# A Fourier mixing and SwiGLU kernel: rising rows turned by copies inside DRAM, the long set in blocks of four rows, and a new table of units

## The chip, the core and the metric

The kernel runs on one core of a Trainium2 chip. Its engines each take their instructions in order: TensorE (PE, matmuls, with its weight loads shown as PEld), VectorE (DVE), ScalarE (ACT), GpSimd (POOL), and SyncE (SP), which here only issues DMAs. ACT and POOL issue a few DMAs too. Matmul results land in PSUM, everything else lies in SBUF (128 partitions) or in DRAM. The metric is the device time of one execution in microseconds (us); less is better.

## What is computed

```python
def _attn_ref(x):                       # x: 8 x 3008 x 256, float32
    X = np.fft.fft(x, axis=1)
    X = np.fft.fft(X, axis=2)
    return X.real.astype(np.float32)

def _moe_ref(x, w_gate, w_val, w_out):  # x: 24064 x 256; w_gate, w_val: 256 x 1536; w_out: 1536 x 256
    g = x @ w_gate
    silu = g * (1.0 / (1.0 + np.exp(-g)))
    val = x @ w_val
    return (silu * val @ w_out).astype(np.float32)
```

The second function gets the 8 x 3008 rows of the first.

## The kernel before

**The mathematics.** The input is real, so output row k and its mirror 3008 - k come from the same two numbers: an even part P and an odd part Q, as P + Q and P - Q. The transform along the 256 columns is folded into the weights (tables `CD` and `SDt`, which give `Wp` and `Wq` from the gate and value weights; `Wm` holds the multiple of `Wq` that turns a plus sum in PSUM into the mirror's sum). The transform along the 3008 rows is halved several times: rows that rise from a quarter's start are added to rows that fall from its end. POOL does these additions (`fold_steps`, L171 to L205), and what is left is a product with the tables `Tab` (`transform_parts`, L1394).

**Sets of rows.** Of every quarter of a batch (752 rows) 188 pairs rise and 188 fall. 128 pairs make the long set A (buffer `XA`, 128 partitions x 8 x 2 x 256 float32; slots 0 to 3 for the four rising quarters, 4 to 7 for the falling ones) and 60 pairs the short set C (buffer `XC`, two batches in its two halves). There is one buffer of each, so a set of a later batch is loaded when the one before it is folded. A falling row's address runs against its partner's. The partitions are therefore filled in blocks: within a block of `LA` (or `LC`) rows the rising pairs go up, and the blocks themselves go down. A falling quarter is one DMA (`down_set`, L142), and a rising set takes one DMA for each block (`up_block`, L140 and L155), to 8 partitions at a time for A (16 DMAs) and 4 for C (15). The tables follow the order of rows (`m_cols`, `putA`), which is why `LA` appears there too. Batch 1 is special: its short set is spread over both halves of `XC` (L164; L169 is a copy from `XC` to `XC`), one parity of the pairs in each, so that six folding steps do for it where a full buffer takes twelve. Its long set's buffer first holds raw weights and the odd tables (`Wraw`, `rrO`), so the loads wait for the readers of these.

**Tiles and units.** 12032 columns of P and Q make 24 tiles, of 480, 512, 512, 480, 512, 512, then seventeen of 512, and one of 320. Each tile has 12 units, one for each 128 columns of the 1536. A unit makes a plus gate and a plus value and, by a further matmul into the same PSUM banks, the mirror's gate and value (L972). ACT takes the Silu (L1084, L1156, L1159), and DVE or POOL the products (`hp` at L1186 and L1192, `hm` for the mirror at L1183, two units at a time on POOL). `hp` and `hm` go to the output product (L1236), whose result ACT evicts (L1243) and SP stores (L1249).

**Kinds of units.** `KINDS` has a row for each tile and a digit for each unit (`w`: both signs' products whole, on DVE, in the first tile and the start of the second). Bit 1 (seeded): ACT writes the row term into PSUM before the value matmul (`v`, L1045) and copies the even value out (`es`, L1107); without it DVE does both in one instruction (`es`, L1109). Bit 2 (split gate): DVE makes the even gate (L1088) and the mirror gate (L1152), and the gate takes two matmuls; without it three. Digit 4 and up: ACT copies the value (`pp`, L1189) and POOL makes the plus product (L1192) instead of DVE (L1186); from 8 up POOL makes the mirror value too (L1195).

**The order of the work.** A planner inside the kernel (`Sched`) lists every operation behind the setup with an engine, a cost and a due time, plays it through and emits each engine's instructions in the order that it finds. Due times are TensorE's running sum plus a shift for each kind of operation (`SHIFT`) and a correction for each tile and kind (`BIAS_ROWS`, 24 rows of 17 numbers). So a change of costs, loads or corrections changes the order on all engines. Loads go to SP in small lots, a few at every unit, mixed with the stores and with the two DMAs that spread a tile's row term over the partitions (`br`, `bc`).

Of the kernel before, what the change touches and what calls it, by code (L numbers as in the profile page):

```python
# [12 lines left out]
F32 = mybir.dt.float32  # L13
# [6 lines left out]
def kernel(  # L20
# [8 lines left out]
    nc = tc.nc  # L29
    B, M, D = x.shape  # L30
    Dff = moe_w_gate.shape[1]
    P = 128
# [3 lines left out]
    R = M // 4  # L36
# [16 lines left out]
    NCR = GH - P  # L53
# [52 lines left out]
    XC = const.tile([P, 8, 2, D], F32, name="XC")  # L106
# [24 lines left out]

    JA, JC = P - LA + 1, GH - LC + 1

    C1_EARLY = 6
    C1_ORDER = "uuduuduuduuduumuueuueuece"
    A1_ORDER = "uuuuduuuuduuuuduuuud"

    def load_a(b, q):
        X3 = XA.rearrange("p a q d -> p a (q d)")
        res = ([lambda h=h: q.dma_start(out=X3[LA * h:LA * (h + 1), 0:4, :],  # L140
                                         in_=up_block(b, JA - LA * h, LA)) for h in range(NA)] +
                [lambda a=a: q.dma_start(out=X3[:, 4 + a, :], in_=down_set(b, a, JA, LA, NA)) for a in range(4)])  # L142
        return in_order(A1_ORDER, u=res[:NA], d=res[NA:]) if b == 1 else res

    def in_order(order, **todo):
        todo = {k: list(v) for k, v in todo.items()}
        return [todo[k].pop(0) for k in order]

    def load_c(b, q):

        X3 = XC.rearrange("p a q d -> p a (q d)")
        p0 = 64 * (b % 2)
        pm = p0 + NCR
        r = slice(p0, p0 + NCR)
        ups = [lambda h=h: q.dma_start(out=X3[p0 + LC * h:p0 + LC * (h + 1), 0:4, :],  # L155
                                       in_=up_block(b, JC - LC * h, LC)) for h in range(NC_)]
        mid = [lambda: q.dma_start(out=XC[pm:pm + 1, 0:4, 1],
                                   in_=rows_at(b, 0, [[R * D, 1], [R * D, 4], [1, D]]))]
        if b != 1:
            return ups + [lambda a=a: q.dma_start(out=X3[r, 4 + a, :], in_=down_set(b, a, JC, LC, NC_))  # L160
                          for a in range(4)] + mid

        def down(a, k):
            q.dma_start(out=XC[0:NCR, 4 + a, 0] if k else XC[r, 4 + a, 0],  # L164
                        in_=rows_at(b, R * (a + 1) - 2 * JC + k, [[2 * LC * D, NC_], [-2 * D, LC], [1, D]]))

        downs = [[lambda a=a, k=k: down(a, k) for a in range(4)] for k in range(2)]
        return in_order(C1_ORDER, u=ups, d=downs[0], e=downs[1], m=mid,
                        c=[lambda: q.dma_start(out=XC[0:NCR, 0:4, 1], in_=XC[r, 0:4, 0])])  # L169
# [82 lines left out]
    q = nc.sync  # L252
# [104 lines left out]
    sc = 2.0 * math.pi * (1.0 - 2e-7)  # L357
# [28 lines left out]
    def load_w(c, only):  # L386
        for i, src in ((0, moe_w_gate), (1, moe_w_val)):
            if i not in only:
# [13 lines left out]
                        in_=rows_at(0, 0, [[2 * R * D, 2], [R * D, 2], [1, D]]))  # L402
# [141 lines left out]
    for hi in range(2):  # L544
        q.dma_start(out=X3c[64 * hi + NCR:64 * hi + 64, :].rearrange("p (c d) -> p c d", d=D),
                    in_=zeros[64 * hi + NCR:64 * hi + 64].unsqueeze(1).to_broadcast([64 - NCR, 16, D]))
    loads_c1 = load_c(1, q)
    for load in loads_c1[:C1_EARLY]:
        load()
# [142 lines left out]
    A1_LOAD = 8  # L692
    ROW_1 = 12
    ROW_2 = 24
    ROW_3 = 35
    LOAD_AT = 2
# [45 lines left out]
    )  # L742
    BIAS = {(t, k): v for t, row in enumerate(BIAS_ROWS) for k, v in zip(SHIFT, row)}
# [11 lines left out]
    W_AT = (0.0, 2.0, 3.2, 4.6)  # L755
# [164 lines left out]
    def pool_us(n):  # L920
# [9 lines left out]
        "06ww20001013",  # L930
        "031303160011",
        "000010312133",
        "010210112012",
        "10110b103133",
        "001601031052",
        "300171700001",
        "331213005030",
        "010271031001",
        "34130b310300",
        "01b300700101",  # L940
        "21312101b300",
        "001371310011",
        "32120011b212",
        "10130b135030",
        "000135003170",
        "033170001011",
        "213b21011200",
        "103b10319610",
        "4030b13300b0",
        "616404563200",  # L950
        "143034169230",
        "706150233313",
# [21 lines left out]
    S = Sched()  # L974
# [310 lines left out]
    for b in range(2, B, 2):  # L1285
        u = slot[(b, 0)] - 1
# [6 lines left out]
    act_at = {}  # L1293
    spread_at = {}
    loads = []

    def run_loads(n):
        for what, k, fn in loads[:n]:
            up = k < (NA if what[0] == "A" else NC_)
            r, w, us, ring = [], [((what[0],), k)], 0.4 if up else 0.62, 0.57 if up or what[0] == "C" else 1.14  # L1300
            if what == ("A", 1):
                r = [(("C",), C1_ORDER.rindex("u"))]
                us, ring = (0.42, 0.75) if A1_ORDER[k] == "u" else (0.75, 1.1)
            if what == ("C", 1):
                us, ring = (0.48, 0.75) if C1_ORDER[k] == "u" else (0.95, 1.0)
                if C1_ORDER[k] == "c":
                    r = [(("C",), j) for j, o in enumerate(C1_ORDER) if o == "u"]
            S.add("SP", us, fn, r=r, w=w, after=[(("A",), "pre" if A1_ORDER[k] == "d" else "preW")] if what == ("A", 1) else [],
                  lat=2.5, ring=ring)
        del loads[:n]  # L1310
# [4 lines left out]
    def fold_step(what, i, unit):  # L1315
        kind, b = what
        q, j = (1, i) if what == ("C", 1) else divmod(i, 6)
        if i == 0:
            run_loads(max((k + 1 for k, (w_, _, _) in enumerate(loads) if w_ == what), default=0))
# [14 lines left out]
        r = {0: [((kind,), k) for k in range(40)], 1: [(tmp, "F")], 2: [(tmp, "F")], 3: [(tmp, "E"), (tmp, "O")],  # L1334
# [4 lines left out]
        if q == 1 and j == 0:  # L1339
            act_at.setdefault(max(unit + LOAD_AT, 15), []).append(what)  # L1340
# [6 lines left out]
    def load_next(what):  # L1347
        kind, b = what
        if kind == "A":
            if b + 1 < B:  # L1350
                loads.extend((("A", b + 1), k, fn) for k, fn in enumerate(load_a(b + 1, nc.sync)))
        else:
            b = b // 2 * 2 + 2
            if b < B:
                loads.extend((("C", b), k, fn) for k, fn in enumerate(load_c(b, nc.sync) + load_c(b + 1, nc.sync)))
# [248 lines left out]
    for k in range(C1_EARLY):  # L1604
        S.add("DMA", 0.01, lambda: None, w=[(("C",), k)], lat=2.0)
# [3 lines left out]
    S.add("DMA", 0.01, lambda: None, w=[(("pq", 0), "Q")], lat=0.1)  # L1609
# [7 lines left out]
    for i, u in enumerate(units):  # L1617
        t, f = u
# [3 lines left out]
        if i == 1:  # L1622
            loads.extend((("C", 1), k, fn) for k, fn in enumerate(loads_c1) if k >= C1_EARLY)
        if i == A1_LOAD:
            loads[0:0] = ((("A", 1), k, fn) for k, fn in enumerate(load_a(1, nc.sync)))
# [41 lines left out]
    S.run({'DVE': 1.6, 'ACT': 1.0, 'POOL': 1.4, 'PE': 0.0, 'SP': 2.0})  # L1667
# [30 lines left out]
```

## Time and profile before

| | us |
|---|---|
| median of three runs | 599.71 |
| lowest and highest | 597.59, 600.29 |
| the profiled execution | 600.4 |
| its span, first to last instruction | 598.6 |

| engine | busy in the span | instructions |
|---|---|---|
| PE | 587.0 (98%) | 3953 |
| DVE | 570.3 (95%) | 1064 |
| ACT | 557.4 (93%) | 1080 |
| POOL | 527.8 (88%) | 486 |

The hardware profiler recorded one execution. A row of a group names the line, the engine, the operation, what is written and read, how often, the busy time, the mean of one in ns, and the idle time just before such instructions with what ended it. A row of the waits names the engine and line that waited, what released it, the total in us, the number of times and the longest. A row of the timeline has the start, the duration, engine, line, operation and operands. In the table by stretches each engine's busy time is followed by its number of instructions, and at the end stand TensorE's granted clock, the mean busy share of 16 DMA engines and GB/s. Some matmul records are missing, and the end of a matmul is modelled.

### The profile page before, as it was taken

How to read it: one execution, taken by the hardware profiler on the slowest of the kernel's cores; microseconds unless marked ns; L12 is line 12 of the kernel's file. 1: busy time of each engine (PE TensorE's matmuls, PEld its weight loads, DVE VectorE, ACT ScalarE, POOL GpSimd, SP SyncE). 2: the span in 40 equal slices, each digit the busy share in tenths (PEclk: the TensorE clock that was granted, in tenths of full speed). 3: DMA queues.
4: the chain of work that ended last, by engine and by line, in shares of the span. 5: the costliest groups of instructions: out<-in, count | busy, mean ns of one | idle time of the engine just before them, and what ended most of it. 6: DMA issues, size and time to landing. Idle time of an engine off the chain costs nothing.

```text
span 598.6 us, 12468 instructions
## 1 busy us (share of the span) xinstructions
PE 587.0 (98%) x3953; PEld 389.2 (65%) x4012; DVE 570.3 (95%) x1064; ACT 557.4 (93%) x1080; POOL 527.8 (88%) x486
## 2 busy tenths in 40 slices
PE   7999999999999999999999999999999999999997
PEld 5456666666666666666666666666666666666686
DVE  8989999999999999999999999999999999999993
ACT  8778989989998999999999999999999999999995
POOL 8977999999899999998999998897986868687772
PEclk9999999999999999999999999999999999999999
DMA  9956347454715523454127122046221202111212
GB/s 247 150 110 115 109 121 141 132 140 117 178 46 107 136 70 113 123 129 138 57 55 166 46 62 82 19 115 161 63 64 37 65 19 80 48 46 53 60 54 81
DMA packets 51082, 57.65 MB, mean 96 GB/s; under 512 B 7283, under 2 KB 38439, under 8 KB 51017
## 3 DMA queue, kind: packets, MB, share of 16 engines
q1 hardware_dynamic: 47433, 53.91, 35.2%
q0 software_dynamic: 3216, 2.36, 2.8%
q8 instruction: 31, 0.51, 0.4%
q10 hardware_dynamic: 368, 0.59, 0.3%
q14 instruction: 34, 0.28, 0.2%
HBM read 29.43 MB, written 24.65 MB: 90 GB/s over the span
## 4 chain that ended last, share of the span: by engine, by line
PE 71%; ACT 8%; DMA 6%; DVE 4%; POOL 3%; issue 3%; SPq 1%; ACTq 0%; POOLq 0%; DVEq 0%
PE o L1236 30%; PE g L972 19%; PE v L972 16%; DMA XA<-in_x_dram 5%; ACT sv L1159 2%; PE o L1394 2%; PE g L1394 2%; ACT v L1045 2%; ACT es L1107 1%; POOL hm L1183 1%; DVE sv L1175 1%; ACT sp L1084 1%; DVE hp L1186 1%; ACT sp L1156 1%; ACT ev L1243 1%
## 5 line engine op out<-in xcount | busy, mean ns | idle before, releaser
L1183 POOL TENSOR_TENSOR hm<-sv 128x1024 bf16<-128x1024 f32 (+2 forms) x137 | 254.7, 1862 | 44.1 <-ACT sv L1159 17.7
L1175 DVE SCALAR_TENSOR_TENSOR sv<-es,v 128x512 f32<-128x512 f32 (+2 forms) x262 | 173.6, 668 | 5.4 <-PE v L972 2.8
L1236 PE MATMUL o<-Wo,hm 128*128 128x256 bf16 (+1 forms) x1128 | 163.6, 273 | 0.3
L1236 PE MATMUL o<-Wo,hp 128*128 128x256 bf16 (+1 forms) x1104 | 159.7, 273 | 0.2
L1186 DVE TENSOR_TENSOR hp<-sp,v 128x512 bf16<-128x512 f32 (+2 forms) x233 | 154.2, 668 | 2.8 <-PE v L972 2.0
L1236 PEld LDWEIGHTS <-hm 128*128 128x128 bf16 (+2 forms) x1140 | 111.8, 98 | 57.9 <-issue 2.5
L1236 PEld LDWEIGHTS <-hp 128*128 128x128 bf16 (+2 forms) x1140 | 111.9, 98 | 55.8 <-issue 0.9
L1159 ACT ACTIVATE sv<-g 128x512 f32<-128x512 f32 (+2 forms) x179 | 116.7, 671 | 4.6 <-PE g L972 2.3
L1084 ACT ACTIVATE sp<-g 128x512 f32<-128x512 f32 (+2 forms) x179 | 110.5, 621 | 4.1 <-PE g L972 2.7
L972 PE MATMUL v<-Pt,Wp 128*128 128x512 bf16 (+2 forms) x288 | 105.4, 375 | 1.8 <-DVE hp L1186 0.5
L972 PE MATMUL g<-Pt,Wp 128*128 128x512 bf16 (+2 forms) x280 | 104.4, 374 | 0.9 <-ACT sv L1159 0.7
L1045 ACT ACTIVATE v<-bc,w 128x512 f32<-128x512 bf16 (+2 forms) x146 | 104.6, 717 | 0.4
L1109 DVE SCALAR_TENSOR_TENSOR es<-bc,w,v 128x512 f32<-128x512 bf16 (+2 forms) x128 | 92.6, 731 | 2.4 <-ACT bc L1595 0.8
L1107 ACT ACTIVATE es<-v 128x512 f32<-128x512 f32 (+2 forms) x146 | 90.0, 618 | 3.8 <-PE g L972 1.0
L972 PE MATMUL g<-Qt,Wq 128*128 128x512 bf16 (+2 forms) x247 | 90.5, 374 | 0.4
L972 PEld LDWEIGHTS <-Wp 128*128 128x128 bf16 x576 | 56.3, 98 | 27.8 <-DVE Wp L505 0.7
L972 PE MATMUL g<-Qt,Wm 128*128 128x512 bf16 (+2 forms) x186 | 69.8, 375 | 0.2
L1088 DVE SCALAR_TENSOR_TENSOR sg<-bc,w,g 128x512 f32<-128x512 bf16 (+2 forms) x95 | 68.4, 723 | 1.4 <-PE g L972 0.7
L1159 ACT ACTIVATE sv<-sg 128x512 f32<-128x512 f32 (+2 forms) x95 | 65.1, 692 | 0.2 <-DVE sg L1152 0.2
L1152 DVE SCALAR_TENSOR_TENSOR sg<-sg,g 128x512 f32<-128x512 f32 (+2 forms) x95 | 62.9, 662 | 1.5 <-PE g L972 0.8
L1156 ACT ACTIVATE sp<-g 128x512 f32<-128x512 f32 (+2 forms) x95 | 57.7, 608 | 5.5 <-DVE sg L1152 5.3
L972 PE MATMUL v<-Qt,Wm 128*128 128x512 bf16 (+2 forms) x159 | 59.4, 374 | 0.8 <-ACT es L1107 0.4
(218 smaller groups left out, 759.1 us busy)
## 6 DMA issues: line engine op xcount, KB each, us to landing
out_dram<-ev SPq DMA_DIRECT2D x96, 128.0 KB
XA<-in_x_dram SPq DMA_DIRECT2D x30, 256.0 KB
XA<-in_x_dram SPq DMA_DIRECT2D x112, 64.0 KB
XC<-in_x_dram SPq DMA_DIRECT2D x28, 120.0 KB
XC<-in_x_dram SPq DMA_DIRECT2D x105, 32.0 KB
bc<-br SPq DMA_DIRECT2D x19, 128.0 KB
St<-Fc SPq DMA_DIRECT2D x12, 128.5 KB
out_dram<-ev SPq DMA_DIRECT2D x12, 120.0 KB
```

The source lines that it names most:

```text
L972: nc.tensor.matmul(ps[:, :n], Wt[:, gv, fs], src[:, :n], start=start, stop=stop, skip_group_check=True)
L1045: nc.scalar.activation(T_[kv][:, :w], bc[t][:, :w], AF.Copy, scale=w0[:, 1, f:f + 1])
L1084: nc.scalar.activation(sp_to()[:, :w], T_[kg][:, :w], AF.Silu)
L1088: nc.vector.scalar_tensor_tensor(T_[keg][:, :w], bc[t][:, :w], w0[:, 0, f:f + 1], T_[kg][:, :w], op0=Alu.mult, op1=Alu.add)
L1107: nc.scalar.activation(T_[kes][:, :w], T_[kv][:, :w], AF.Copy, scale=2.0 if on_pool(u) > 1 else 1.0)
L1109: nc.vector.scalar_tensor_tensor(T_[kes][:, :w], bc[t][:, :w], w0[:, 1, f:f + 1], T_[kv][:, :w], op0=Alu.mult, op1=Alu.add)
L1156: nc.scalar.activation(sp_to()[:, :wp], T_[kg][:, :wp], AF.Silu)
L1159: nc.scalar.activation(sv()[:, f % 2, w - 1::-1, 1], T_[kgm if by_dve else kg][:, :w], AF.Silu)
L1175: nc.vector.scalar_tensor_tensor(sv()[:, f % 2, w - 1::-1, 0], T_[kes][:, :w], 2.0, T_[kv][:, :w], op0=Alu.mult, op1=Alu.subtract)
L1183: nc.gpsimd.tensor_tensor(hts_(t)[1][:, f - 1:f + 1, :w], sv()[:, :, :w, 1], sv()[:, :, :w, 0], op=Alu.mult)
L1186: nc.vector.tensor_tensor(hts_(t)[0][:, f, :wp], T_[ksp][:, :wp], T_[kv][:, :wp], op=Alu.mult)
L1236: nc.tensor.matmul(st["ps"][:n, j, :], hts[t][minus][:, f, c:c + n], Wo[:, f, :], start=(f == 0), stop=(f == nF - 1))
```

## The change

Six things change together.

1. `LA` goes from 8 to 4: the long set lies in 32 blocks of 4 rows.
2. For batches 1 to 7 the rising rows of each quarter are first copied inside DRAM (`reorder`) into a buffer in which the blocks lie in the order of the partitions: 4 copies of 256 KB for A, 4 of 120 KB for C. The loads then read that buffer (`reordered`): two of 512 KB for A, one of 480 KB for C. The falling rows are loaded as before.
3. Batch 1's short set is loaded without the copy inside `XC`: one load for each parity from the buffer. The falling rows come first, then the copies.
4. The planner issues the copies of batches 2 and 3 from unit 11 on, one for each unit, and those of later batches from unit 26 on, one for every third unit; the loads wait for them. It is also told new times for the start: batch 1's short set at hand after 17.0, the copies of its long set after 18.0, raw weights slightly later, and SP free from 12.0.
5. `KINDS` has other digits in 18 rows: 139 units are seeded (146 before), 93 have a split gate (95), 46 give the plus product to POOL (41); 12 mirror values on POOL as before.
6. `BIAS_ROWS` is replaced, all 24 rows.

```diff
-    LA, NA = 8, P // 8
+    LA, NA = 4, P // 4
...
+    def reorder(kind, b, q):
+        n, L, N, j0 = (P, LA, NA, JA) if kind == "A" else (NCR, LC, NC_, JC)
+        t = scratch[kind, b] = dram.tile([4, N, 2 * L, D], F32, name=f"t{kind}{b}")
+
+        def one(a):
+            q.dma_start(out=t[a].rearrange("h r d -> r h d"),
+                        in_=rows_at(b, R * a + 2 * j0 - 1, [[D, 2 * L], [-2 * L * D, N], [1, D]]))
+
+        return [lambda a=a: one(a) for a in range(4)]
+
+    def reordered(kind, b, a0, a1):
+        return scratch[kind, b][a0:a1].rearrange("a h (i q) d -> (h i) a (q d)", q=2)
...
-        res = ([lambda h=h: q.dma_start(out=X3[LA * h:LA * (h + 1), 0:4, :],
-                                         in_=up_block(b, JA - LA * h, LA)) for h in range(NA)] +
+        return ([lambda a=a: q.dma_start(out=X3[:, a:a + 2, :], in_=reordered("A", b, a, a + 2)) for a in (0, 2)] +
                 [lambda a=a: q.dma_start(out=X3[:, 4 + a, :], in_=down_set(b, a, JA, LA, NA)) for a in range(4)])
...
+        return ([lambda: q.dma_start(out=X3[r, 0:4, :], in_=reordered("C", b, 0, 4))] +
+                [lambda a=a: q.dma_start(out=X3[r, 4 + a, :], in_=down_set(b, a, JC, LC, NC_)) for a in range(4)] +
+                [lambda: mid_c(b, q)])
...
+    def up_c1(k, q):
+        q.dma_start(out=XC[slice(64, 64 + NCR) if k else slice(0, NCR), 0:4, 1],
+                    in_=scratch["C", 1][:].rearrange("a h (i q) d -> q (h i) a d", q=2)[k])
...
-    loads_c1 = load_c(1, q)
-    for load in loads_c1[:C1_EARLY]:
-        load()
+    clear_c(1)
+    for k in range(2):
+        for a in range(4):
+            down_c1(a, k, q)
+        if not k:
+            clear_c(0)
+    early = reorder("C", 1, q) + reorder("A", 1, q)
+    for fn in early[:5]:
+        fn()
+    mid_c(1, q)
+    up_c1(1, q)
+    up_c1(0, q)
+    for fn in early[5:]:
+        fn()
...
-    W_AT = (0.0, 2.0, 3.2, 4.6)
+    W_AT = (0.0, 2.3, 3.4, 4.6)
...
-        "06ww20001013",
-        "031303160011",
-        "000010312133",
+        "60ww24000310",
+        "031310330010",
+        "000031313300",
...
+        if i % (1 if i < 26 else 3) == 0 and i > 10:
+            for todo in pending[:1]:
+                del pending[:1]
+                issue(*todo)
+        if i == 26:
+            for b in range(4, B + 2, 2):
+                for ch_, b_ in (("C", b), ("C", b + 1), ("A", b - 1), ("A", b)):
+                    pending.extend(reorder_ops(ch_, b_) if b_ < B else [])
```

In the order that the planner then emits, the setup of TensorE, up to its 460th instruction, stays as it was. POOL folds batch 1's short set ahead of the four copies of odd tables rather than behind three of them, and it has eight mirror products and two plus products between there and the last coefficients of batch 1's first half, where it had seven and one. TensorE has the equivalent of eight 512-column matmuls more ahead of batch 1's first transform.

More of the change, by code (lines that the diff above doesn't have):

```diff
@@ L145, in in_order, with mid_c @@
-    def in_order(order, **todo):
-        todo = {k: list(v) for k, v in todo.items()}
-        return [todo[k].pop(0) for k in order]
+    def mid_c(b, q):
+        pm = 64 * (b % 2) + NCR
+        q.dma_start(out=XC[pm:pm + 1, 0:4, 1], in_=rows_at(b, 0, [[R * D, 1], [R * D, 4], [1, D]]))
     def load_c(b, q):
         X3 = XC.rearrange("p a q d -> p a (q d)")
[L152 to L169, printed above, removed]
@@ L1318, in fold_step @@
         if i == 0:
[L1319 removed]
+            run_loads(max((k + 1 for k, (w_, _, _) in enumerate(loads) if w_ == what or kind == w_[0] == "C" and w_[1] == b + 1), default=0))
         def fn():
@@ L1603 @@
     S.hold("st", 0)
-    for k in range(C1_EARLY):
-        S.add("DMA", 0.01, lambda: None, w=[(("C",), k)], lat=2.0)
+    S.add("DMA", 0.01, lambda: None, w=[(("C",), 7)], lat=C1_AT_HAND)
+    for k in range(4):
+        S.add("DMA", 0.01, lambda: None, w=[(("sc", "A", 1), k)], lat=A1_TURNED)
     for fc in (1, 2):
```

101 lines of the change are left out of this document (59 added, 42 removed), and 24 rows, old and new, of the table BIAS_ROWS.

## The prediction

> **What bounds the kernel now.** I read the engine totals first, then the busy time by stretches, and then TensorE's own waits.
>
> ```profile
> span 598.6 us, 12468 instructions
> PE 587.0 (98%) x3953; PEld 389.2 (65%) x4012; DVE 570.3 (95%) x1064; ACT 557.4 (93%) x1080; POOL 527.8 (88%) x486
> ```
>
> ```profile
> core 0: us, PE busy (x) PEld busy (x) DVE busy (x) ACT busy (x) POOL busy (x), PEclk, DMA share, GB/s
> 0.00:19.00 19.00, 15.91 (x104) 10.00 (x106) 16.56 (x69) 14.73 (x25) 17.43 (x40) 1.00 0.89 220
> 19.00:25.00 6.00, 5.76 (x28) 2.36 (x25) 5.66 (x15) 4.68 (x10) 4.84 (x9) 1.00 0.89 153
> 25.00:125.00 100.00, 97.83 (x648) 62.48 (x657) 94.20 (x168) 87.01 (x170) 92.75 (x98) 1.00 0.57 125
> 125.00:575.00 450.00, 447.26 (x3007) 297.46 (x3054) 440.16 (x785) 434.79 (x837) 403.12 (x333) 1.00 0.33 85
> 575.00:598.60 23.60, 20.27 (x174) 16.90 (x171) 13.72 (x32) 16.16 (x42) 9.69 (x9) 0.98 0.24 73
> ```
>
> PE is idle 3.09 us in the setup (19.00 less 15.91), 0.24 in the next six, 2.17 in the hundred after, 2.74 in the 450 us behind them and 3.33 in the last stretch, mostly the last eviction and store. At full clock it is idle 0.6% of the longest stretch; part of even that is matmul records missing from the trace. So the end is set by PE's work, and no way of loading can win more than the idle 2.17 + 2.74 = 4.9 us plus what it spares PE itself. PE's longest waits name their cause:
>
> ```profile
> PE g L972 <- ACT sv L1159: 0.7, 1, 0.7
> PE v L972 <- DVE hp L1186: 0.5, 1, 0.5
> PE v L972 <- ACT es L1107: 0.4, 1, 0.4
> PE v L972 <- DVE Wp L505: 0.2, 1, 0.2
> ```
>
> Left out above are three waits of 1.0 us in the setup, ahead of the change. None of the four names a load or POOL. But POOL, which folds the loaded rows, does wait for loads, twice:
>
> ```profile
> POOL SDf L178 <- DMA XA<-in_x_dram: 2.1, 1, 2.1
> POOL SDf L178 <- DMA out_dram<-ev: 2.0, 1, 2.0
> ```
>
> ```profile
> 36.95 0.73 POOL L1541 MEMSET Tab<- 64x756 bf16 x1
> ...
> 42.33 2.36 POOL L178 TENSOR_TENSOR SDf<-XC 128x1020 f32<-128x1020 f32 x1 [2.06 <-DMA XA<-in_x_dram]
> ...
> 55.72 1.89 POOL L1183 TENSOR_TENSOR hm<-sv 128x1024 bf16<-128x1024 f32 x1 [0.72 <-DVE sv L1175]
> 59.65 2.36 POOL L178 TENSOR_TENSOR SDf<-XA 128x1020 f32<-128x1020 f32 x1 [2.03 <-DMA out_dram<-ev]
> ...
> 83.54 0.64 POOL L192 TENSOR_TENSOR CEa<-Af 128x258 bf16<-128x258 f32 x1
> ...
> 84.66 0.33 PE L1394 MATMUL g<-Tab,CEa 128*128 128x189 bf16 x2
> ```
>
> These are batch 1's folds: the short set at 42.33, the long set at 59.65, and the last coefficients of the first half at 84.18 (83.54 + 0.64), half a microsecond before PE takes them at 84.66, without a recorded wait. This is the only place where a load comes near to setting PE's time.
>
> **PE's work.** Counted over the kinds in the two unit tables: 146 seeded units become 139, 95 split gates 93, 41 plus products on POOL 46; 12 mirror values stay there. A gate that is no longer split needs one 512-column matmul more.
>
> ```profile
> 23.57 0.86 PE o L1442 x4
> ```
>
> The chain of waits has such a matmul at 0.86 / 4 = 0.215 us, so two cost **+0.43 us**, with nothing to hide behind on the busiest engine.
>
> **The other engines.** Means of one instruction:
>
> ```profile
> L1186 DVE TENSOR_TENSOR hp<-sp,v 128x512 bf16<-128x512 f32 (+2 forms) x233 | 154.2, 668 | 2.8 <-PE v L972 2.0
> L1045 ACT ACTIVATE v<-bc,w 128x512 f32<-128x512 bf16 (+2 forms) x146 | 104.6, 717 | 0.4
> L1109 DVE SCALAR_TENSOR_TENSOR es<-bc,w,v 128x512 f32<-128x512 bf16 (+2 forms) x128 | 92.6, 731 | 2.4 <-ACT bc L1595 0.8
> L1107 ACT ACTIVATE es<-v 128x512 f32<-128x512 f32 (+2 forms) x146 | 90.0, 618 | 3.8 <-PE g L972 1.0 <-PE v L972 1.0 <-DVE sv L1175 0.9
> L1088 DVE SCALAR_TENSOR_TENSOR sg<-bc,w,g 128x512 f32<-128x512 bf16 (+2 forms) x95 | 68.4, 723 | 1.4 <-PE g L972 0.7 <-PE o L1236 0.5
> L1152 DVE SCALAR_TENSOR_TENSOR sg<-sg,g 128x512 f32<-128x512 f32 (+2 forms) x95 | 62.9, 662 | 1.5 <-PE g L972 0.8
> L1192 POOL TENSOR_TENSOR hp<-sp,pp 128x512 bf16<-128x512 f32 (+1 forms) x41 | 51.2, 1251 | 4.4 <-ACT pp L1189 2.3 <-ACT sp L1156 1.9
> L1189 ACT COPY pp<-v 128x512 f32<-128x512 f32 (+1 forms) x41 | 24.9, 608 | 3.6 <-DVE sv L1175 3.1 <-PE v L972 0.3
> ```
>
> ACT loses 7 x (0.717 + 0.618) and gains 5 x 0.608: -6.3 us. DVE gains 7 x 0.731 and loses 2 x (0.723 + 0.662) and 5 x 0.668: -1.0. POOL gains 5 x 1.251: +6.3. I cost all three at nothing: between 125 and 575 us ACT is idle 15.2 us, DVE 9.8, POOL 46.9. Only PE's 0.43 is on the path. Were POOL's cover gone, its 6.3 us would show, spread over the tiles that got a product more (by the tables, net two before tile 11 and three behind it).
>
> **The loads.** SP's 631 issues become 491: 217 rising loads, each to 8 or 4 partitions, and one copy inside XC give way to 56 copies inside DRAM and 22 loads from there. That is time on SP, not on PE; behind SP's queue stand the stores and the bias rows, which get shorter queues. What counts is when batch 1's sets arrive.
>
> ```profile
> 13.92 1.50 SPq L545 DMA_DIRECT2D XC<-Z  x2
> 15.46 3.69 SPq L155 DMA_DIRECT2D XC<-in_x_dram  x2
> 19.19 0.92 SPq L164 DMA_DIRECT2D XC<-in_x_dram  x1
> ...
> 37.94 1.42 SPq L140 DMA_DIRECT2D XA<-in_x_dram  x4
> ...
> 52.45 0.54 SPq L142 DMA_DIRECT2D XA<-in_x_dram  x1
> ```
>
> Before, the long set's 20 loads go out from 37.94 to 52.99 and POOL has them at 59.65: 2 MB in 21.7 us. After, SP first issues two clears (1.50) and eight falling loads (0.92 each): the copies of the short set start at about 13.92 + 1.50 + 7.4 = 22.8 us. The trace shows no copy from DRAM to DRAM. Nearest below: a 60-row issue, 0.92; above: the 3.69 of two issues that were held up, 1.85 each. I take 0.92 and, for landing, the 6.7 us from the last issue to POOL's start (59.65 less 52.99). Four copies then land at 22.8 + 3.7 + 6.7 = 33 us, the two loads behind them 6.7 us later, at 40. The long set's buffer is also used by tables; their last reader is here:
>
> ```profile
> L372 ACT ACTIVATE Tab<-XA,zero x2: 599/614/629, 31.5 to 33.5; 128x376 bf16<-128x376 f32 x2
> ...
> 13.00:38.00 25.00, 24.64 (x147) 12.17 (x148) 21.96 (x53) 19.10 (x39) 22.39 (x42) 1.00 0.80 134
> ```
>
> So it can fill from 34.1 on; 2 MB take 15.6 us at that stretch's 134 GB/s, 9.5 at the 220 of the setup: in place at 44 to 50.
>
> When does POOL want them? Its order after: the short set's fold comes ahead of the four table copies, and one more mirror product (1.862 us) and one more plus product (1.251) stand before the last coefficients.
>
> ```profile
> L1183 POOL TENSOR_TENSOR hm<-sv 128x1024 bf16<-128x1024 f32 (+2 forms) x137 | 254.7, 1862 | 44.1 <-ACT sv L1159 17.7 <-DVE sv L1175 16.1 <-ACT sp L1084 2.9
> L1546 POOL COPY Tab<-Tab 64x752 bf16<-64x752 bf16 x4 | 3.3, 817 | 0.2
> ```
>
> It is free at 37.68 (36.95 + 0.73). Before, 42.33 to 84.18 held 39.1 us of work (41.85 less the waits of 2.03 and 0.72). After: 39.1 + 3 x 0.817 + 1.862 + 1.251 = 44.7, so 82.4 us without waits; the long set is wanted at 52.8 (37.68, plus 57.61 - 42.33 - 0.72, plus three copies, less one mirror product). On PE eight 512-column matmuls more, 1.7 us, stand before the transform, at 84.66 + 1.7 = 86.4, less what gaps go. POOL goes from half a microsecond ahead to about 3 ahead; a short set that lands only at 40 takes 2.3 of these.
>
> That does not remove PE's waits by itself, as those name ACT and DVE. I credit half of the 2.17 us in 25:125, **-1.1** (bounds 0 and -2.2): a POOL that isn't late frees the mirror buffers earlier. For 125:575 the whole order of units changes; bounds are -2.7 (all idle gone) and +2.5 (one wait as long as POOL's longest on an sv, below); I take **0**, as nothing in these stretches prefers a side.
>
> ```profile
> POOL hm L1183 <- ACT sv L1159: 17.7, 11, 2.5
> ```
>
> Sum against the profiled execution, 600.4 us (span 598.6 and 1.8 around it): 600.4 + 0.43 - 1.1 = 599.7. That execution lies 0.7 above the median of 599.71, so the forecast for a median is **599.0 us**: no change that can be told.
>
> **Rivals.** *All idle goes* (24%). The new order leaves PE no wait behind the setup: 600.4 + 0.43 - 4.9 - 0.7 = 595.2. From 596.7 down it counts as faster, which needs 2.3 of the 3.8 us that my sum leaves. For it: ACT and DVE, which PE's waits name, get less work. Against: PE's listed waits there are single and short, and a reshuffled order makes new ones.
>
> *The long set comes late* (24%). The copies, the short set's loads and the long set's loads stand in SP's one queue, and a load now waits for a copy to land. If the set lands at 59.65 as before, POOL stands 59.65 - 52.8 = 6.8 us, less the 3 it is ahead: 3.8 us on PE, 600.4 + 0.43 + 3.8 - 0.7 = 603.9. It decides from a landing at about 56. For it: DMA share 0.80 in 13:38, and 1.5 MB more to copy there. Against: 2 large issues in place of 16.
>
> [...]
>
> *The loads matter to nothing* (10%). PE's waits stay as they were: 600.4 + 0.43 - 0.7 = 600.1. For it: no wait of PE names a load.
>
> **How the numbers follow.** My own case has 42%, with its range from 597.9 (all of 2.17 gone) to 602.6 (none gone and a wait of 2.5 us). About 0.5%, 3 us, is what a measurement of this kernel tells from no change; the bounds are 596.7 and 602.7. Faster is the first rival, 0.24; slower the second, 0.24; within them 0.42 + 0.10 = 0.52. The range for 8 in 10 reaches towards both rivals, 595.8 to 604.0.
>
> **What would show it.** Right: 5 more plus products on POOL, 2 more gate matmuls; POOL's waits at the first folds of XC and XA gone; the long set's fold starting at about 53 us and the first transform of batch 1 at 85 to 86 without a wait; PE idle 25:125 about 1 us. Wrong: a POOL wait at the fold of XA with PE waiting near 85 us (second rival); PE idle under 1 us over 25:575 (first); new PE waits of microseconds behind 125 us, which I have put at zero; a setup longer than 19 us.

## The result, and the profile after

| | before | after |
|---|---|---|
| median, us (20 runs each) | 599.79 | 597.66 |
| lowest and highest | 597.59, 601.94 | 597.20, 598.90 |
| span of the profiled execution | 598.6 | 596.0 |

The ratio of the times is 0.9966, with an interval of 0.9958 to 0.9973: 2.1 us less, a third of a per cent. That lies within the 0.5% that the prediction calls no change, and in the forecast's range. The forecast of 599.0 had the direction and a third of the size (0.7 of 2.1). Of the runs below, one is left out of its ratio: 886.62 us, among twelve of the kernel with the old order and the new loads, whose other eleven took 597.43 to 598.16.

The engine totals of the kernel after:

```profile
span 596.0 us, 12394 instructions
PE 590.9 (99%) x4014; PEld 390.6 (66%) x4014; DVE 568.6 (95%) x1062; ACT 553.6 (93%) x1071; POOL 533.5 (90%) x491
```

Its busy time by stretches, with the columns as before, and behind it all of TensorE's recorded waits of the kernel after:

```profile
25.00:125.00 100.00, 100.00 (x674) 64.22 (x673) 96.22 (x173) 87.29 (x172) 96.01 (x101) 1.00 0.67 188
125.00:575.00 450.00, 449.99 (x3061) 297.89 (x3060) 438.16 (x783) 433.21 (x833) 406.39 (x336) 1.00 0.32 95
```

```profile
PE o L306 <- DVE sel L258: 1.0, 1, 1.0
PE v L1015 <- DVE Wp L508: 0.2, 1, 0.2
```

Both waits stand in or at the end of the setup. From 25 to 575 us the profile shows no gap of PE: it is busy for 549.99 of 550 us. What is left to win there is PE's own work.

To see where the 2.6 us between the two spans went, take the first matmul of the first unit and the last matmul of all, in the timelines of before and then of after:

```profile
18.86 0.57 PE L972 MATMUL g<-Pt,Wp 128*128 128x480 bf16 x2
...
593.78 1.50 PE L1236 MATMUL g<-Wo,hm 128*64 128x256 bf16 x12
```

```profile
18.20 0.57 PE L1015 MATMUL g<-Pt,Wp 128*128 128x480 bf16 x2
...
590.87 1.50 PE L1279 MATMUL g<-Wo,hm 128*64 128x256 bf16 x12
```

| part | before | after | difference |
|---|---|---|---|
| setup, up to the first unit | 18.86 | 18.20 | -0.66 |
| first unit to the end of the last matmul | 576.42 | 574.17 | -2.25 |
| behind it, to the end of the span | 3.35 | 3.60 | +0.25 |

Together -2.66, the spans' 2.6 but for rounding. In the middle part 0.43 us of matmuls were added by the count of units; if they cost that, 2.7 us of gaps or slack went.

POOL's first folds of batch 1 and the first transform, in the timeline of after:

```profile
39.17 2.35 POOL L181 TENSOR_TENSOR SDf<-XC 128x1020 f32<-128x1020 f32 x1 [1.95 <-DVE hp L1053]
...
54.32 2.36 POOL L181 TENSOR_TENSOR SDf<-XA 128x1020 f32<-128x1020 f32 x1 [0.21 <-DMA out_dram<-ev]
...
83.17 0.65 POOL L195 TENSOR_TENSOR CEa<-Af 128x258 bf16<-128x258 f32 x1
...
84.03 0.33 PE L1453 MATMUL o<-Tab,CEa 128*128 128x189 bf16 x2
```

The long set is folded at 54.32 instead of 59.65, with 0.21 us of waiting instead of 2.03. The short set is still waited for, 1.95 us; the row names a product of DVE, which the fold doesn't read, and the loads from the buffer, issued up to here, are the likelier cause:

```profile
24.00 3.47 SPq L142 DMA_DIRECT2D tC<-in_x_dram  x4
...
34.36 0.84 SPq L171 DMA_DIRECT2D XC<-tC  x2
...
40.80 1.87 SPq L152 DMA_DIRECT2D XA<-tA  x2
```

POOL has the last coefficients at 83.17 + 0.65 = 83.82, and PE takes them at 84.03: 0.2 us later, where the prediction gave POOL 3 us, less up to 2.3 for a late short set.

### The profile page after: what moved, and what is told of

Read it like the earlier page. It is cut to its first block, busy times and chain, and to the rows that moved or that the text cites. A ratio compares the mean times of both kernels' runs of the same rounds, so it can differ in the third digit from the quotient of the medians.

```text
span 596.0 us, 12394 instructions
## 1 busy us (share of the span) xinstructions
PE 590.9 (99%) x4014; PEld 390.6 (66%) x4014; DVE 568.6 (95%) x1062; ACT 553.6 (93%) x1071; POOL 533.5 (90%) x491
## 3 DMA queue, kind: packets, MB, share of 16 engines
q0 software_dynamic: 3216, 2.36, 2.9%
## 4 chain that ended last, share of the span: by engine, by line
PE 96%; DVE 0%; ACT 0%; issue 0%
PE o L1279 41%; PE g L1015 27%; PE v L1015 21%; PE g L1453 2%; PE o L1453 2%; PE v L1279 1%; PE o L1501 1%; PE g L622 0%; PE o L622 0%; PE g L1279 0%; PE o L1582 0%; PE g L1650 0%; DVE Wp L508 0%; ACT es L1289 0%; DVE Qt L646 0%
## 5 line engine op out<-in xcount | busy, mean ns | idle before, releaser
L1226 POOL TENSOR_TENSOR hm<-sv 128x1024 bf16<-128x1024 f32 (+2 forms) x137 | 254.7, 1862 | 32.3 <-ACT sv L1202 12.9
L1229 DVE TENSOR_TENSOR hp<-sp,v 128x512 bf16<-128x512 f32 (+2 forms) x228 | 151.6, 671 | 1.9 <-PE v L1015 1.1
L1127 ACT ACTIVATE sp<-g 128x512 f32<-128x512 f32 (+2 forms) x181 | 112.1, 621 | 5.9 <-PE g L1015 4.0
L1015 PE MATMUL g<-Pt,Wp 128*128 128x512 bf16 (+2 forms) x288 | 107.5, 374 | 0.0
L1015 PE MATMUL g<-Qt,Wq 128*128 128x512 bf16 (+2 forms) x288 | 105.4, 375 | 0.1
L1088 ACT ACTIVATE v<-bc,w 128x512 f32<-128x512 bf16 (+2 forms) x139 | 100.3, 726 | 1.9 <-DVE sv L1218 1.0
L1152 DVE SCALAR_TENSOR_TENSOR es<-bc,w,v 128x512 f32<-128x512 bf16 (+2 forms) x135 | 97.9, 732 | 2.1
L1150 ACT ACTIVATE es<-v 128x512 f32<-128x512 f32 (+2 forms) x139 | 86.0, 621 | 3.2 <-PE v L1015 1.6
L1015 PE MATMUL g<-Qt,Wm 128*128 128x512 bf16 (+2 forms) x195 | 73.1, 376 | 0.0
L1235 POOL TENSOR_TENSOR hp<-sp,pp 128x512 bf16<-128x512 f32 (+1 forms) x46 | 57.2, 1245 | 8.0 <-ACT pp L1232 7.8
L1015 PEld LDWEIGHTS <-Wq 128*128 128x128 bf16 x437 | 42.7, 98 | 27.5 <-issue 0.4
```

Of the source, the lines that this page charges most:

```text
L1015: nc.tensor.matmul(ps[:, :n], Wt[:, gv, fs], src[:, :n], start=start, stop=stop, skip_group_check=True)
L1088: nc.scalar.activation(T_[kv][:, :w], bc[t][:, :w], AF.Copy, scale=w0[:, 1, f:f + 1])
L1127: nc.scalar.activation(sp_to()[:, :w], T_[kg][:, :w], AF.Silu)
L1150: nc.scalar.activation(T_[kes][:, :w], T_[kv][:, :w], AF.Copy, scale=2.0 if on_pool(u) > 1 else 1.0)
L1152: nc.vector.scalar_tensor_tensor(T_[kes][:, :w], bc[t][:, :w], w0[:, 1, f:f + 1], T_[kv][:, :w], op0=Alu.mult, op1=Alu.add)
L1226: nc.gpsimd.tensor_tensor(hts_(t)[1][:, f - 1:f + 1, :w], sv()[:, :, :w, 1], sv()[:, :, :w, 0], op=Alu.mult)
```

## The experiments

Two theories stood against each other. By the first the gain comes from the loads: batch 1's sets land sooner, and a wait goes. By the second it comes from the order: the new unit table and corrections let the planner emit a schedule without gaps. The change of block length was a third suspect, as it touches the loads of the setup too.

**One half of the change at a time.** First the kernel after with the unit table and corrections of before (all of both tables; the first rows shown):

```diff
-        "60ww24000310",
-        "031310330010",
-        "000031313300",
+        "06ww20001013",
+        "031303160011",
+        "000010312133",
...
```

> The changed kernel's loads and blocks of 4 rows with the unit table and the corrections of before. Theory A (the loads: batch 1's sets land earlier, POOL no longer stands for the long set, and TensorE's waits in 25:125 go with it): most of the 2.1 us stays, TensorE idles under 1 us in 25:125, ratio about 0.996. Theory B (the order: the new unit table and corrections are what took out the waits): the gain is gone or worse, since the old corrections were made for other loads, TensorE idles 2 us or more in 25:575 and the ratio is 1.000 or above.

Then the kernel before with the two tables of after, the same rows the other way round:

```diff
-        "06ww20001013",
+        "60ww24000310",
...
```

> The kernel before (16 and 15 rising loads, blocks of 8 rows) with the new unit table and corrections. Theory A: no gain; the long set lands at about 59 us as before, POOL stands for it, TensorE waits as before or more and does two matmuls more, ratio 1.001 or above. Theory B: most of the gain comes, ratio about 0.997.

Neither did what a sum of parts would: new loads with old tables took 609.12 us, ratio 1.0161 (1.0146 to 1.0176), old loads with new tables 614.88, ratio 1.0264 (1.0245 to 1.0282). Both are slower than both originals. The busy time by stretches of the first:

```profile
25.00:125.00 100.00, 100.00 (x673) 64.15 (x672) 96.20 (x173) 89.34 (x174) 95.47 (x100) 1.00 0.65 180
125.00:575.00 450.00, 444.43 (x2972) 288.64 (x2970) 429.58 (x765) 424.90 (x813) 393.43 (x326) 1.00 0.32 95
```

With the new loads there is no gap in 25:125, as the loads theory wants; what it loses it loses behind 125 us, where PE does 2972 matmuls against 3061 in the same time. In the other kernel, with the loads of before, POOL waits 2.4 us for them, but PE's gap in 25:125 is only 0.48 us (2.17 in before), so what a late load costs depends on the order too. Behind 125 us PE does 2948 matmuls there:

```profile
125.00:575.00 450.00, 443.24 (x2948) 286.09 (x2947) 425.55 (x757) 419.53 (x801) 395.85 (x328) 1.00 0.32 83
```

So these two runs can't tell the parts' worth. The planner made a third and a fourth order, and these have gaps of their own. To measure the loads alone the order has to be held.

**The load's lateness alone, order held.** The kernel before, whose order of instructions stays as it was on every engine, but batch 1's long set brings only the first 16 of each pair's 512 values, so that it lands sooner. The rest of that set isn't loaded.

```diff
+        n = 16 if b == 1 else 2 * D
-        res = ([lambda h=h: q.dma_start(out=X3[LA * h:LA * (h + 1), 0:4, :],
-                                         in_=up_block(b, JA - LA * h, LA)) for h in range(NA)] +
+        res = ([lambda h=h: q.dma_start(out=X3[LA * h:LA * (h + 1), 0:4, 0:n],
+                                         in_=rows_at(b, 2 * (JA - LA * h) - 1, [[2 * D, LA], [R * D, 4], [1, n]])) for h in range(NA)] +
...
```

> The kernel before, with the order on every engine unchanged; of batch 1's long set only the first 16 of each 512 values are loaded, the rest of its buffer keeps batch 0's values, so that the 20 DMAs carry 1/32 of the bytes. Theory A in its strict form (POOL's stand of 2.0 us for the long set makes TensorE's waits in 25:125): the stand goes and TensorE's idle in 25:125 falls from 2.17 to about 1 us or less, ratio 0.998. Theory B (those waits lie in the order of ACT and DVE): POOL's stand goes, TensorE's waits stay, ratio 1.000.

Measured: 598.63 us, ratio 0.9986 (0.9977 to 0.9995); span 596.7, from before's 598.6. The gain in the medians is 0.8 (by the interval, 0.3 to 1.4) and in the spans 1.9, because before's profiled execution, at 600.4, lies 1.0 above the 599.43 that before has beside this run. Stretches, and the timeline:

```profile
25.00:125.00 100.00, 100.00 (x671) 63.96 (x670) 96.20 (x173) 89.43 (x174) 94.81 (x99) 1.00 0.42 106
125.00:575.00 450.00, 449.99 (x3059) 297.69 (x3058) 439.74 (x784) 434.74 (x838) 403.10 (x333) 1.00 0.32 85
```

```profile
19.12 0.57 PE L974 MATMUL g<-Pt,Wp 128*128 128x480 bf16 x2
...
57.82 2.36 POOL L180 TENSOR_TENSOR SDf<-XA 128x1020 f32<-128x1020 f32 x1
...
122.55 0.60 PE L1238 MATMUL o<-Wo,hp 128*96 128x256 bf16 x4
...
591.85 1.50 PE L1238 MATMUL g<-Wo,hm 128*64 128x256 bf16 x12
```

From first unit to last matmul it takes 593.35 - 19.12 = 574.23 us, 2.19 less than before, with not one instruction moved: the 2.17 that PE was idle between 25 and 125 us. Taking away the load's lateness takes away PE's gaps. This run's short set was folded earlier too, 21.66 us behind the first unit instead of 23.47. To see which of the two counts, take the same matmuls in both timelines, from the first unit on:

| PE's matmul in before, at | behind the first unit | with the shortened load | lost |
|---|---|---|---|
| 59.98 | 41.12 | 41.10 | 0.02 |
| 64.74 | 45.88 | 45.00 | 0.88 |
| 80.86 | 62.00 | 60.55 | 1.45 |
| 107.25 | 88.39 | 86.05 | 2.34 |

POOL is level as well at its last product ahead of the long set (36.86 and 36.85 us behind the first unit), and 2.09 late from that set's fold on. So all of the loss comes behind the long set's fold, in steps. How, the timeline of before shows:

```profile
59.65 2.36 POOL L178 TENSOR_TENSOR SDf<-XA 128x1020 f32<-128x1020 f32 x1 [2.03 <-DMA out_dram<-ev]
...
62.11 1.90 POOL L1183 TENSOR_TENSOR hm<-sv 128x1024 bf16<-128x1024 f32 x1
...
64.05 0.64 ACT L1159 ACTIVATE sv<-g 128x512 f32<-128x512 f32 x1 [0.88 <-PE g L1591]
...
64.74 0.38 PE L972 MATMUL g<-Pt,Wp 128*128 128x512 bf16 x1 [0.70 <-ACT sv L1159]
...
78.93 1.29 DVE L1175 SCALAR_TENSOR_TENSOR sv<-es,v 128x512 f32<-128x512 f32 x2 [0.71 <-POOL hm L1183]
...
80.86 0.38 PE L972 MATMUL v<-Pt,Wp 128*128 128x512 bf16 x1 [0.55 <-DVE hp L1186]
...
124.63 0.60 PE L1236 MATMUL o<-Wo,hp 128*96 128x256 bf16 x4
```

The mirror product at 62.11 stands behind the fold in POOL's order, and starts 0.10 us after the fold's end (59.65 + 2.36); with the twelve copies below, where POOL stands for 9.46 us ahead of the fold, it comes behind it too, at 67.66. When the product at 62.11 ends, at 64.01, ACT writes the next `sv`, which needs a buffer that such a product has read, and PE, which needs the PSUM that ACT reads, goes on 0.05 us after ACT is done. ACT's row names a matmul here, which starts at 63.66 and ends at the same time as the product, at 64.04. With the shortened load ACT's instruction is under way at 62.79, before that matmul starts at 63.91, so it doesn't wait for the matmul; and in the run with twelve copies below, where the wait is longer, such an instruction names the mirror product. PE's row names ACT; the cause is a DMA, two engines further back. The step at 80.86 goes through DVE: its `sv` at 78.93 waits 0.71 us for a late mirror product, and PE for the product behind it.

The same rows settle another point. The same output product (the first with 128*96) begins 124.63 - 18.86 = 105.77 us behind the first unit in before and 122.55 - 19.12 = 103.43 here: all of the gain is made by then (2.34, of which 0.15 is lost again later). Behind it both take the same time, 470.65 and 470.80 us to the end of the last matmul. So before's 2.74 us of "idle" between 125 and 575 us were no time lost but missing records: 3007 matmuls are recorded there, against 3059 of the same program here.

**The new loads in the old order.** The instructions of PE, DVE, ACT and POOL stay exactly in the order of before, with its tables; loads and blocks are those of after, put in the places of the old rising loads, with nothing issued in the places left over.

```diff
+            return in_order(A1_ORDER, u=ups + [none] * 14, d=downs)
+        return reorder("A", b, q) + [none] * 10 + ups + downs
...
```

> The changed kernel's loads (copies inside DRAM, blocks of 4 rows, batch 1's sets first) in the kernel before, with the order of TensorE, VectorE, ScalarE and GpSimd kept exactly as before: the planner still sees the old rising loads, and in their places stand the copies, the loads from them, or nothing. Theory A (the loads alone take TensorE's waits out of 25:125 and shorten the setup): first unit at 18.2 to 18.4 us, no idle in 25:125, from the first unit to the last matmul 574 us, ratio 0.996 or a little less, as TensorE has two matmuls fewer than in the changed kernel. Theory B (the new units and corrections are part of the gain): ratio 0.998 or above.

597.51 us, ratio 0.9975 (0.9963 to 0.9986). To compare it closely with the kernel after, both were run again side by side, unchanged:

> The changed kernel once more, beside the next one on the same chip. If the loads make the whole gain: first unit at about 18.2 us, no idle in 25:125, and a time within 0.5 us of the kernel with the old order and the new loads (which has two matmuls fewer, 0.43 us). If the new units and corrections add something: over 0.5 us less than that kernel.

> The old order with the new loads once more, beside the changed kernel on the same chip. If the loads make the whole gain: the same time or up to 0.5 us less. If the new units and corrections add something: over 0.5 us more.

After: 597.76, ratio 0.9969 (0.9956 to 0.9983). The old order with the new loads: 597.68, ratio 0.9969 (0.9958 to 0.9981). Stretches and timeline of the latter:

```profile
25.00:125.00 100.00, 100.00 (x674) 64.23 (x672) 96.21 (x173) 89.41 (x174) 95.20 (x100) 1.00 0.62 166
125.00:575.00 450.00, 449.99 (x3059) 297.90 (x3058) 439.69 (x786) 434.65 (x839) 402.52 (x333) 1.00 0.34 100
```

```profile
18.18 0.57 PE L1007 MATMUL g<-Pt,Wp 128*128 128x480 bf16 x2
...
590.60 1.50 PE L1271 MATMUL g<-Wo,hm 128*64 128x256 bf16 x12
```

The loads with their blocks give the whole gain: 0.9969 by either order. From first unit to last matmul it is 592.10 - 18.18 = 573.92 us, against 574.17 of after in one profile and 573.62 in the second. In the times the new units and corrections are worth nothing that can be measured, and no version tried beats the kernel after by more than the runs differ.

**The length of the blocks.** After with blocks of 8 rows, no engine's order changed:

```diff
-    LA, NA = 4, P // 4
+    LA, NA = 8, P // 8
```

> The changed kernel with LA back at 8: 16 blocks of 8 rows; the copies of the long set then have 16 rows outermost instead of 8. The order on every engine stays. Both theories: the same time as the changed kernel, ratio 0.9966 within 0.001, as nothing that TensorE waits for moves. [...] Rival: the blocks of 4 rows matter for the setup, whose first unit starts 0.66 us earlier in the changed kernel; then this kernel loses about 0.6 us.

598.23 us, ratio 0.9978 (0.9967 to 0.9990), which overlaps with the interval of after, so the time doesn't separate them. POOL's wait at the short set's fold stays, 2.0 us; that set's copies go by `LC`, which is 4 in both. PE's timeline does show a difference, in the setup, where PE waits for batch 0's first loads, as it did in the kernel before. With blocks of 8, and then in after:

```profile
11.04 1.95 PE L438 MATMUL o<-XC,putC 128*128 128x512 f32 x4 [0.73 <-DMA XC<-in_x_dram]
```

```profile
10.36 1.94 PE L438 MATMUL o<-XC,putC 128*128 128x512 f32 x4
```

With blocks of 8 the first unit starts at 18.64. And the reverse, before with blocks of 4. As its rising rows go block by block, a set now takes 32 loads, so that only its setup is to be read:

```diff
-    LA, NA = 8, P // 8
+    LA, NA = 4, P // 4
...
-    A1_ORDER = "uuuuduuuuduuuuduuuud"
+    A1_ORDER = "uuuuuuuud" * 4
```

> The kernel before with blocks of 4 rows and so 32 rising loads for each long set; its order behind the setup is another one, so only the setup is read. If the blocks shorten the setup: first unit at 18.2 to 18.4 us, without TensorE's wait for the first load of XA. If not: 18.6 to 19.1 us, as in the four runs with blocks of 8 rows.

It took 643.35 us in one run, and its first unit starts at 18.35.

Over all profiles the first unit starts at 18.18 to 18.36 us with blocks of 4 (seven profiles; an eighth, below, at 20.82), and at 18.64 to 19.30 with blocks of 8 (five). The matmuls on batch 0's rows in `XC`, shown above, start at 10.36 to 10.52 in those seven and at 11.04 to 11.71 in those five. So the 0.66 us of the setup go mostly with the blocks, not with the copies; the two runs that change `LA` move the first unit by 0.44 and 0.51. PE reads the rising rows there, and these come by one DMA whatever the block length; ahead of it stand the falling rows of `XA`, which lie in such blocks. Why the load behind them is used sooner with shorter blocks stays open.

**The long set made late.** After with spare copies of 256 KB on SP ahead of batch 1's two loads of the long set; the copies' result isn't read. First six:

```diff
+        def up(a):
+            if b == 1 and a == 0:
+                for i in range(6):
+                    spare = dram.tile([4 * 2 * LA, NA, D], F32, name=f"spare{i}")
+                    q.dma_start(out=spare[0:2 * LA], in_=rows_at(7, 2 * JA - 1, [[D, 2 * LA], [-2 * LA * D, NA], [1, D]]))
+            q.dma_start(out=X3[:, a:a + 2, :], in_=reordered("A", b, a, a + 2))
...
```

> The changed kernel with six more copies of 256 KB inside DRAM (to spare space, of batch 7's rows) ahead of the loads of batch 1's long set, the order of the other engines unchanged. The second rival of the prediction: from a landing of about 56 us TensorE waits as long as the set is late. By the rate of the setup's stretches, 160 to 250 GB/s, six copies take 6 to 10 us; the set is then used at 56 to 60 us instead of 54.3, TensorE loses up to 5 us, ratio 0.997 to 1.005. [...] If TensorE has room there after all: 0.9966 whatever the landing.

603.82 us, ratio 1.0071 (1.0047 to 1.0094). In its timeline the fold waits, and then PE:

```profile
59.65 2.35 POOL L188 TENSOR_TENSOR SDf<-XA 128x1020 f32<-128x1020 f32 x1 [2.85 <-DMA XA<-tA]
...
65.30 0.38 PE L1022 MATMUL v<-Pt,Wp 128*128 128x512 bf16 x1 [2.45 <-ACT v L1095]
```

Its first unit starts at 20.82, 2.6 us late, and the spare copies, issued from 43 us on, can't be the cause. Seven of PE's first eight matmuls on batch 0's rows took nearly twice as long as in after. The same two of them in this run, and then in after:

```profile
9.51 1.91 PE L445 MATMUL g<-XA,putA 128*128 128x512 f32 x2
```

```profile
8.19 1.02 PE L438 MATMUL g<-XA,putA 128*128 128x512 f32 x2
```

Most take 1.06 us there, and 0.59 in after; the granted clock of 0 to 19 us is 1.00 in both. They start at 5.97 (6.13 in after), and the ones on `XC` behind them at 12.97 (10.36), so the 2.6 us are lost there, where PE's matmuls are recorded with nearly twice their length. Why it did so is not known; the four runs of this kernel lie within 0.8 us, so they seem to share it. It accounts for about 2.6 of the 6.1 us that this kernel takes more than after.

Because of this, twelve copies were tried, once with each block length, in case the copies' shape sets their pace (`range(12)`, and `LA = 8` in the second):

> The changed kernel with twelve spare copies ahead of batch 1's long set instead of six; only the landing is read (POOL's wait at the first fold of XA) and what TensorE waits from there. If lateness passes on whole: TensorE's idle in 25:125 is POOL's delay against the changed kernel, counted from the first unit in both. [...]

> The same with blocks of 8 rows, so that each copy has 16 rows outermost. [...]

610.67 us with blocks of 4 and 604.60 with blocks of 8, one run each. The timeline of the one with blocks of 4:

```profile
41.12 14.66 SPq L156 DMA_DIRECT2D spare<-in_x_dram  x12
...
65.20 2.35 POOL L188 TENSOR_TENSOR SDf<-XA 128x1020 f32<-128x1020 f32 x1 [9.46 <-DMA tC<-in_x_dram]
...
69.58 0.64 ACT L1209 ACTIVATE sv<-g 128x512 f32<-128x512 f32 x1 [10.86 <-POOL hm L1233]
...
70.84 0.59 PE L1022 MATMUL v<-Pt,Wp 128*128 128x512 bf16 x1 [10.80 <-ACT v L1095]
```

And of the one with blocks of 8:

```profile
41.57 7.75 SPq L156 DMA_DIRECT2D spare<-in_x_dram  x12
...
60.15 2.35 POOL L188 TENSOR_TENSOR SDf<-XA 128x1020 f32<-128x1020 f32 x1 [5.79 <-DMA tC<-in_x_dram]
...
65.79 0.38 PE L1022 MATMUL v<-Pt,Wp 128*128 128x512 bf16 x1 [4.42 <-ACT v L1095]
```

Measured from each kernel's first unit (20.82, 19.30 and 18.20):

| kernel | long set's fold | later than after | PE's wait |
|---|---|---|---|
| after | 36.12 | | none |
| six copies | 38.83 | 2.71 | 2.45 |
| twelve, blocks of 8 | 40.85 | 4.73 | 4.42 |
| twelve, blocks of 4 | 47.00 | 10.88 | 10.80 |

Each microsecond that the fold comes late is one that PE stands, but for 0.1 to 0.3 us. PE goes on 5.6 us behind the fold's start in all three, once the mirror product behind the fold and two instructions of ACT are done. At the transform, some 25 us later, nothing more is lost: with six copies PE is as far behind after there as at 65.30 (2.37 and 2.36 us, counted from the first unit).

## Why the prediction came out as it did

**The number: in the range, in part by its width.** The sum for the profiled execution was 599.7, and the profiled execution of after took 597.77, 1.9 us less: 1.1 of gaps, 0.66 of setup and 0.43 of matmuls that don't show, less 0.25 behind the last matmul. The range of the prediction's own case began at 597.9, so the median of 597.66 lies just outside it; the whole range holds it since it reached towards both rivals.

**Right: PE's work is the bound.** DVE, ACT and POOL changed by -1.7, -3.8 and +5.7 us of busy time (forecast -1.0, -6.3 and +6.3), and in the order kept from before, without any of this, the time is the same.

**Right: when things come.** The copies were forecast to start at 22.8 and to land at 33; they start at 24.00, 0.87 us each (0.92 was taken), and the loads behind them leave at 34.36. The short set was given for 40 and is folded at 39.17; the long set was wanted at 52.8 and is folded at 54.32. When it landed the trace doesn't show, only that it was there by then. From the short set's fold to the last coefficients POOL takes 44.65 us (44.7 was given, without waits). The first transform was given for 86.4 less what gaps go, 85 to 86, and comes at 84.03: 86.4 less 0.66 of setup and less the 1.70 us that PE had lost in before by its matmul at 83.71.

**Wrong: "None of the four names a load or POOL", and with it half of 2.17.** This was the step that failed. The term for the gaps of 25:125 was -1.1 between bounds of 0 and -2.2. In the profiled execution it is -2.2: all of it goes as soon as the load is early, as the shortened load showed with the order unchanged. The prediction did name the mechanism (a POOL that isn't late frees the mirror buffers earlier), but took half for it, since the waits were read one step deep. The row that showed the link was the mirror product behind POOL's fold, whose end at 64.01 releases ACT at 64.05. The third rival (the loads matter to nothing) falls with it. How much of this a usual execution of before loses is less sure: in the medians the shortened load gains 0.8 us, with a setup that was 0.26 longer, so about 1.1.

**Wrong: the setup at zero.** The sum has no term for it; it was -0.66, most of which goes with the blocks of 4. This was listed only as something that could get longer.

**Not seen: +0.43 for two more matmuls.** That was taken as having nothing to hide behind. From first unit to last matmul after takes 574.17 and 573.62 us in its two profiles; 0.45 of the 0.55 between them arise inside the first unit, before its first value matmul (19.50 and 19.03). From that value matmul to the end of the last one the new order takes 572.87, 572.77 and 572.90 us (after, its second profile, blocks of 8), and the old order with early loads 573.12, 573.07 and 573.13 (the new loads twice, the shortened load). So the new order is 0.2 to 0.4 us shorter there, not 0.43 longer; what it gains elsewhere isn't known, and the medians (597.76 and 597.68 side by side) don't show it.

**Right in value, wrong in its bounds: 0 for 125:575.** "All idle gone" counted 2.74 us there that were missing records, so the first rival's 595.2 could not be had: what could go was 2.2, not 4.9. The forecast of that rival, corrected by this, is 600.4 + 0.43 - 2.2 - 0.7 = 597.9, and with the setup's 0.66 it is 597.3, next to the measured 597.66; profile against profile, without the 0.7, it is 598.0 and 597.77.

**Wrong: 3 us of room, and a landing at 56 as the point.** The second rival didn't happen, but its price was set too low. Its room was read at the transform near 85 us, where POOL turned out to be only 0.2 us ahead anyway, partly because the short set's wait of 1.95 us stayed. The prediction gave that wait both ways: 2.3 us for a set that lands at 40, and gone among the signs of being right. The room that counts is at the mirror product behind the fold, and is 0.1 to 0.3 us. The point is therefore the fold's own time, 54.3, and behind it PE pays one for one. In after the copies start at 24.00, the loads that read them leave by 42.67, and the fold waits only 0.21 us: the long set is still in time.

**The two tables.** For a new order behind 125 us the bound above was +2.5. It was too low for what a planner can make: the two kernels with half of the change record 5.6 and 6.8 us of gaps there (450 less 444.43 and 443.24), and their times lie 11.5 and 17.2 us above after. That the corrections are fitted to one set of loads and units is an inference from these two runs, not shown by itself.

## What to carry to other kernels

A wait that names the next engine may have its cause several engines away: look what stands behind a late instruction in its engine's order, as the mirror product behind POOL's fold here, and who waits for that. Before idle time is counted as something to win, compare the number of recorded instructions with another execution of the same program, since missing records look like gaps (2.74 us here). And where a planner decides the order, freeze the order to measure a part of the change; swapping one half at a time measured the planner here, by 10 to 15 us, and not the loads' 2.

## What the runs showed of the hardware that was not expected

**The granted clock fell to 0.50 in or behind the two longest waits, 10.80 and 4.42 us.** PE alone by stretches of the kernel with twelve copies in blocks of 4 (busy time, granted clock, DMA share, GB/s):

```profile
60.00:62.00 2.00, 0.04 (x1) 1.00 0.86 315
62.00:64.00 2.00, 0.00 (x0) 0.62 0.53 205
...
76.00:77.00 1.00, 1.00 (x9) 0.93 0.39 98
```

And with blocks of 8:

```profile
66.00:67.00 1.00, 1.00 (x6) 0.63 0.94 318
67.00:68.00 1.00, 1.00 (x5) 0.50 0.58 165
...
69.00:70.00 1.00, 1.00 (x6) 0.67 0.68 208
70.00:71.00 1.00, 1.00 (x11) 1.00 0.94 204
```

The stretches left out in between (64 to 76 and 68 to 69 us) show 0.50. If the clock was either 1.00 or 0.50 in these stretches, their means give as an estimate that in the first it fell at 62.5 and returned at 76.1, 5.3 us after PE restarted at 70.84; in the second it fell at 66.3, when PE (restarted at 65.79) was already at work, and returned at 69.7. At 0.50 a 512-column matmul starts 0.43 us after the one before it (72.49, 72.92, 73.35), at 1.00 0.22 us (57.70, 57.92, 58.13). So the wait cost more than itself: PE, 10.52 us behind the same matmul of after when it restarts at 70.84, is 13.11 behind at 76.90, which is 2.6 us more, half of the 5.3. The span is 608.9 - 596.0 = 12.9 us longer. The kernel with six copies and a wait of 2.45 us keeps 1.00:

```profile
25.00:125.00 100.00, 97.55 (x653) 62.01 (x652) 93.84 (x169) 85.02 (x168) 92.31 (x99) 1.00 0.70 198
```

By this estimate the stretches at 0.50 were 13.7 and 3.4 us long. The first begins 2.4 us after PE's last matmul ahead of the wait, at 60.04, and 8.3 us before it restarts; the second begins when PE has been at work again for 0.5 us. What sets these times the runs don't show.

**Twelve copies with 8 rows outermost ran at half the rate of twelve with 16, 192 against 378 GB/s.** Outermost means the slowest dimension of the copy. The same twelve copies, 3 MB in all, kept SP for 14.66 us with 8 rows outermost and for 7.75 with 16, and the set behind them was folded at 65.20 and 60.15. While they ran, the mean busy share of the 16 DMA engines and the rate (the last two columns) were, first with 8 and then with 16 rows:

```profile
45.00:48.00 3.00, 3.00 (x22) 1.00 0.54 192
```

```profile
45.00:48.00 3.00, 3.00 (x22) 1.00 1.09 378
```

The busy share halves with the rate; which engines a copy used no trace shows. Three copies in a row, issued at 35.7 us in the same two runs, kept SP for 2.03 us with 8 rows and 1.89 with 16, 0.68 and 0.63 each; of the twelve each kept it 1.22 and 0.65 us. In the kernel after itself the 8 rows cost nothing that shows, as the run with blocks of 8 was not faster (598.23 us).
